# High and low words of h alternate in one tile, so that stationary columns lie 8 bytes apart

## The chip, the cores and the metric

One core of a Trainium2 chip runs the whole program. The metric is the device time of one execution in microseconds; for the kernel before, three runs gave a median of 735.1 us (735.01 to 736.07). An execution taken by the hardware profiler is what all rows below come from.

## The reference

Eight batches of 576 query rows and eight heads of width 64 go through two softmax attentions and then a gated feed-forward layer of width 1536 with three weight matrices:

```
p_packed = sm_attn(p, k, v)             # 32 rows per head
out      = sm_attn(q, p_packed, p_packed)
x        = out, as 4608 tokens x 512
g        = x @ w_gate
silu     = g * (1.0 / (1.0 + np.exp(-g)))
return   (silu * (x @ w_val)) @ w_out   # float32, 4608 x 512
```

`sm_attn` subtracts the row maximum, takes exp with scale 1/8, and divides by the sum plus 1e-9. The three weight matrices arrive as float64 and are made float32 on the chip.

## The kernel before

**What is multiplied.** The second attention is not applied to values first. Its probabilities (tile `a2`, 256 packed rows by 576 tokens of one batch) are multiplied with packed values that have gone through the weights (tile `m`). So a chunk of 128 columns of g, and one of the value branch, is m as stationary operand times a2 as moving operand, and comes out with the 128 feed-forward columns on the partitions and 256 or 320 tokens along the free axis. h = silu(g) * value has that layout too: 128 feed-forward columns by 256 tokens, and is the stationary operand of the output product, 128 tokens (columns of h) at a time, with 512 columns of w_out moving.

**High and low words.** To hold precision in TensorE's one-pass type float32r, a factor is split in a high word (the value rounded to float32r) and a low word (the rest). Each product is then three matmuls: low times high, high times low, high times high. For m and a2 the tiles are `mh`, `ml`, `a2h`, `a2l`; for w_out `wo_h`, `wo_l`; for h `hh`, `hl`.

**The loops.** `batch` (L904) runs over batches 1 to 7, and in it over 12 chunks of 128 feed-forward columns, each for a first part of the tokens (a) and a second (b), 256 and 320 columns wide. `gv_chunk` (L619) issues 6 matmuls in each of two PSUM banks (tag gv, two buffers, so a chunk's banks are also the next chunk's). Behind them ScalarE takes silu of the first bank (L640), VectorE multiplies it with the second (L644, for b a 64-column rest too, L647), and `h_split` (L610) makes the two words: ScalarE writes `hh` (the copy at L178), VectorE writes `hl` = h - hh (L614). `out_mm` (L650) multiplies them with w_out, three matmuls for each of two 128-token halves: (hl, wo_h), (hh, wo_l), (hh, wo_h). The output product of a chunk is issued one chunk of the same part later, so between the making of an h and its use stand an output product, the other part's chunk, another output product, and a chunk. The 64-token rests of two batches are collected in `t4`, split by VectorE alone (`split4`, tiles with tag 4, L180 and L614) and multiplied at the end of the odd batch into a bank named aux.

**What sets the order.** TensorE's order is as written (manual). For batch 0 a list of words (`PROGRAM`) sets the order on VectorE, ScalarE and SyncE too; there `h_high` and `h_low` make the words of the last two chunks, and earlier chunks use unsplit float32 (L828). From batch 1 on the attention of the next batches is put between the matmuls by tables (`FIRST`, `LATER`), called through `fill`. Some of these places put short matmuls, 32 columns of stationary operand wide, between a chunk and the output product behind it.

**The tiles that the change touches.** `hh` and `hl` are separate tiles of 128 x 256 float32r, three buffers each (`h_tile`, L607); with tag 4, two buffers each. They stand at consecutive addresses, and a stationary operand is 128 adjacent columns, 512 bytes in a row in each partition.

**Rows with a step of 8 bytes that are there already.** The weights come as pairs of 32-bit words. `f64_convert` (L191) reads high and low words of such pairs with a step of 8 bytes: L197 on ScalarE reads them and writes without gaps, L198 reads and writes with that step, L200 and L201 on VectorE have one operand with it and one without.

Of the kernel before, what the change touches and what calls it, by code (L numbers as in the profile page):

```python
# [11 lines left out]
F32R = mybir.dt.float32r  # L12
# [11 lines left out]
P = 128  # L24
# [108 lines left out]
def tile_pack_attention_swiglu(ctx: ExitStack, tc: tile.TileContext, qT, kT, v, vq, pT, wgv, wout, out):  # L133
# [5 lines left out]
    pool = ctx.enter_context(tc.tile_pool(name="pool", bufs=1))  # L139
# [24 lines left out]
    def pin(ins):  # L164

        return tc.keep_in_program_order(ins) if steady[0] else ins
# [9 lines left out]
    def copy(e, dst, src):  # L176
        if e is nc.scalar:
            e.copy(dst, src)  # L178
        else:
            e.tensor_copy(dst, src)  # L180
# [423 lines left out]

    t4 = {}

    def h_tile(t):  # L607
        return pool.tile([P, 256], F32R, tag=t, bufs=3, name=t)

    def h_split(src, hi, lo, between=lambda: False, tag=""):  # L610
        hh, hl = (pool.tile([P, 256], F32R, tag=t + tag, bufs=2, name=t) if tag else h_tile(t) for t in ("hh", "hl"))
        copy(hi, hh, src)
        last = between()
        low = lo.tensor_tensor(hl, src, hh.bitcast(F32), op=ALU.subtract)  # L614
        if last:
            pin(low)
        return hh, hl

    def gv_chunk(b, fc, is_b, fill, behind, between):  # L619
        odd = b % 2  # L620
        n = NB if is_b else NA
        off = (0 if odd else 256) if is_b else (320 if odd else 0)
        mh, ml = ms[b, fc // 2]
        ah, al = a2[b]
        f = fc % 2
        pgs = []
        for s in range(2):
            pg = ps_gv.tile([P, 512], F32, tag="gv", name="gv")
            pgs.append(pg)
            i = 0  # L630
            for m_, a_ in ((ml, ah), (mh, al), (mh, ah)):
                for g in range(NPAR):
                    nc.tensor.matmul(  # L633
                        pg[:, :n], m_[:, g, f, s * P : (s + 1) * P], a_[:, g, off : off + n],
                        start=(i == 0), stop=(i == 5),
                    )
                    i += 1
            fill()
        sg = pool.tile([P, NB], F32, tag="sg", bufs=1, name="sg")
        nc.scalar.activation(sg[:, :n], pgs[0][:, :n], AF.Silu)  # L640
        behind()
        hf = pool.tile([P, 256], F32, tag="hf", bufs=2, name="hf")
        o, o4 = (64, 0) if is_b and odd else (0, 256)
        nc.vector.tensor_tensor(hf, pgs[1][:, o : o + 256], sg[:, o : o + 256], op=ALU.mult)  # L644
        if is_b:
            r, r4 = slice(64 * odd, 64 * odd + 64), slice(o4, o4 + 64)
            nc.vector.tensor_tensor(t4[b // 2][:, fc, r], pgs[1][:, r4], sg[:, r4], op=ALU.mult)  # L647
        return h_split(hf, nc.scalar, nc.vector, between)
# [70 lines left out]
    with tc.manual_schedule(engines={mybir.EngineType.PE}):  # L719
# [19 lines left out]
        with tc.manual_schedule(  # L739
# [29 lines left out]
            hs = {}  # L769
# [42 lines left out]
                    nc.vector.tensor_tensor(t4[0][:, fc, :64], x[:, r], sg[:, r], op=ALU.mult)  # L812

            def h_high(i):
                hs[i].append(h_tile("hh"))
                nc.scalar.copy(hs[i][1], hs[i][0])

            def h_low(i):
                hs[i].append(h_tile("hl"))
                nc.vector.tensor_tensor(hs[i][2], hs[i][0], hs[i][1].bitcast(F32), op=ALU.subtract)  # L820

            def outs(i):
# [33 lines left out]
            def half_of(f, b):  # L856
# [5 lines left out]

            words = {
                "g": gv, "silu": silu, "h": hmul, "hh": h_high, "hl": h_low, "out": outs,
                "z_scores": lambda x: (None if x else s1_tile(0), s1_scores(0, x)), "z_max": lambda x: s1_max(0, x),
                "z_top": lambda x: s1_top(0), "z_exp": lambda x: s1_exp(0, True), "z_turn": lambda x: s1_turn(0, x),
# [21 lines left out]
            for word in PROGRAM.split():  # L888
                name = word[: word.index(":") + 1] if ":" in word else word.rstrip("0123456789")
# [14 lines left out]
        def batch(b, behind):  # L904
# [47 lines left out]
            def split4(*ks):  # L952
                for k in ks:
                    halves[k] = h_split(
                        t4_t[:, 2 * k : 2 * k + 2].rearrange("p f t -> p (f t)"), nc.vector, nc.vector, tag="4"
                    )
# [64 lines left out]
```

## Time and profile before

| | us |
|---|---|
| Median of three runs | 735.1 |
| The profiled execution, whole | 734.87 |
| Its span, first to last instruction | 733.1 |
| TensorE busy (6242 matmuls) | 723.9 |
| Loads of stationary operands busy (PEld, 6242) | 590.4 |
| VectorE busy | 454.2 |
| ScalarE busy | 373.7 |

So 1.8 us of the execution lie outside the span. TensorE's granted clock was 1.0 in all of it. In the profile's rows PE is a matmul, and PEld the load of its stationary operand, which overlaps the matmul before. Both last longer than the distance to the next one, since they are pipelined: what a matmul costs in a full stream is read from start to start, not from its duration. In the timeline, columns are start and duration in us, engine, line, operation, tile written from tiles read, and shape; a count of x2 merges two instructions. In groups, behind the bar stand busy time in us and mean ns of one, then idle time of the engine before them.

### The profile page before, as it was taken

Reading aid. Unit: us, or ns where it says so; the run is one execution under the profiler, and the core shown is the slowest. Engines: PE = TensorE matmul, PEld = TensorE weight load, DVE = VectorE, ACT = ScalarE, POOL = GpSimd, SP = SyncE. Lnnn points to the kernel's source line nnn. Section 1 sums busy time; section 2 is a strip of 40 time slices with the busy share of each in tenths; the row PEclk is TensorE's granted clock in tenths of the full one; section 3 lists DMA queues with packets and bytes.
Section 4 is the critical chain, followed back from the end, with each engine's and each line's share of the span. In section 5 each row is a group of like instructions: output and inputs, shape, how many; then the busy total and the mean of one; then the engine's idle time right before and its main releaser. Section 6 shows DMA issues by size and latency. Waiting matters only on the chain.

```text
span 733.1 us, 15099 instructions
## 1 busy us (share of the span) xinstructions
PE 723.9 (99%) x6242; PEld 590.4 (81%) x6242; DVE 454.2 (62%) x1009; ACT 373.7 (51%) x668; POOL 2.0 (0%) x13
## 2 busy tenths in 40 slices
PE   8899999999999999999999999999999999999997
PEld 4655667888888888888888888888888888888886
DVE  4999779665755557664764646665574655744333
ACT  3779737754635445553563535654453535533331
POOL 0000000000000000000000000000000000000000
PEclk9999999999999999999999999999999999999999
DMA  9697482310112201302112011102001000010001
GB/s 344 269 346 276 140 315 95 111 73 2 65 58 85 74 1 66 126 4 73 66 48 93 21 57 65 43 19 73 1 2 72 4 2 1 1 59 1 1 1 72
DMA packets 20004, 59.15 MB, mean 81 GB/s; under 512 B 5984, under 2 KB 7008, under 8 KB 17376
## 3 DMA queue, kind: packets, MB, share of 16 engines
q1 hardware_dynamic: 19792, 58.12, 21.9%
q8 instruction: 49, 0.80, 0.5%
q14 instruction: 19, 0.16, 0.1%
q10 hardware_dynamic: 144, 0.07, 0.0%
HBM read 48.69 MB, written 9.49 MB: 79 GB/s over the span
## 4 chain that ended last, share of the span: by engine, by line
PE 96%; DVE 1%; issue 0%; DVEq 0%
PE gv L633 36%; PE acc L652 34%; PE aux L267 7%; PE gv L787 6%; PE acc L828 5%; PE aux L652 4%; PE gv_aux L482 1%; PE gv_aux L398 1%; PE gv_aux L267 1%; DVE w L200 0%; PE acc L726 0%; PE aux L343 0%; DVE w L201 0%; PE aux L324 0%; DVE ot L180 0%; PE aux L398 0%
## 5 line engine op out<-in xcount | busy, mean ns | idle before, releaser
L640 ACT ACTIVATE sg<-gv 128x256 f32<-128x256 f32 (+1 forms) x168 | 69.0, 411 | 175.3 <-PE gv L633 161.6
L644 DVE TENSOR_TENSOR hf<-gv,sg 128x256 f32<-128x256 f32 x168 | 71.0, 422 | 129.8 <-PE gv L633 118.5
L633 PE MATMUL gv<-a2h,ml 128*128 128x256 f32 (+1 forms) x672 | 143.5, 295 | 0.0
L633 PE MATMUL gv<-a2l,mh 128*128 128x256 f32 (+1 forms) x672 | 143.4, 295 | 0.0
L633 PE MATMUL gv<-a2h,mh 128*128 128x256 f32 (+1 forms) x672 | 143.4, 295 | 0.0
L652 PE MATMUL acc<-wo_h,hl 128*128 128x512 f32 x344 | 139.8, 406 | 0.0
L652 PE MATMUL acc<-wo_l,hh 128*128 128x512 f32 x344 | 135.5, 394 | 0.0
L652 PE MATMUL acc<-wo_h,hh 128*128 128x512 f32 x344 | 135.5, 394 | 0.0
L633 PEld LDWEIGHTS gv<-a2h,ml 128*128 128x128 f32 x672 | 116.4, 189 | 15.3 <-ACT sg L803 0.4
L178 ACT CAST hh<-hf 128x256 fp32r<-128x256 f32 x168 | 67.7, 403 | 101.9 <-DVE hf L644 101.8
L633 PEld LDWEIGHTS gv<-a2l,mh 128*128 128x128 f32 x672 | 107.8, 189 | 0.0
L633 PEld LDWEIGHTS gv<-a2h,mh 128*128 128x128 f32 x672 | 107.6, 188 | 0.0
L614 DVE TENSOR_TENSOR hl<-hf,hh 128x256 fp32r<-128x256 f32 x168 | 69.8, 416 | 46.4 <-ACT hh L178 46.3
L652 PEld LDWEIGHTS acc<-wo_h,hl 128*128 128x128 f32 x344 | 64.5, 188 | 28.0 <-issue 19.2
L652 PEld LDWEIGHTS acc<-wo_h,hh 128*128 128x128 f32 x344 | 64.6, 188 | 14.6
L652 PEld LDWEIGHTS acc<-wo_l,hh 128*128 128x128 f32 x344 | 64.6, 188 | 8.3 <-issue 0.2
L571 DVE TENSOR_TENSOR ml<-aux,mh 128x512 fp32r<-128x512 f32 x92 | 58.9, 682 | 5.4 <-ACT mh L597 5.4
L267 PE MATMUL aux<-w,ppt 64*32 64x512 f32 (+1 forms) x784 | 52.1, 588 | 0.9 <-DVE w L201 0.9
L597 ACT CAST mh<-aux 128x512 fp32r<-128x512 f32 x92 | 49.4, 590 | 5.6 <-PE aux L267 1.2
L640 ACT ACT_TABLE_LOAD x30 | 38.5, 1283 | 13.6 <-PE gv L633 9.8
L828 PE MATMUL acc<-wo_f,h 128*128 128x512 f32 x80 | 37.8, 602 | 0.0
L828 PEld LDWEIGHTS acc<-wo_f,h 128*128 128x128 f32 x80 | 14.2, 189 | 16.7 <-issue 16.2
(153 smaller groups left out, 754.3 us busy)
## 6 DMA issues: line engine op xcount, KB each, us to landing
st<-in_wgv SPq DMA_DIRECT2D x12, 1024.0 KB, 7.6
k_t<-in_kT SPq DMA_DIRECT2D x16, 576.0 KB, 4.9
q_t<-in_qT SPq DMA_DIRECT2D x16, 576.0 KB, 4.9
out<-ot SPq DMA_DIRECT2D x36, 256.0 KB, 2.1
v_t<-in_vq SPq DMA_DIRECT2D x6, 1280.0 KB, 5.7
st<-in_wout SPq DMA_DIRECT2D x6, 1024.0 KB, 6.8
v_t<-in_v SPq DMA_DIRECT2D x2, 1024.0 KB, 8.7
p_t<-in_pT SPq DMA_DIRECT2D x7, 64.0 KB, 2.4
```

What stands on the lines that cost most here:

```text
L178: e.copy(dst, src)
L267: nc.tensor.matmul(outs[par][32 * hp : 32 * hp + 32], lhs(r, hp), rhs(r, hp), start=True, stop=True)
L398: nc.tensor.matmul(pss[par][NP * j : NP * j + NP, i * SQ : (i + 1) * SQ], p_t[r, 2 * g + i, :], k_t[r, j // 2, 2 * g + i, j % 2 * SQ : j % ...
L571: pin(nc.vector.tensor_tensor(*lows.pop(0), op=ALU.subtract))
L597: nc.scalar.copy(m[0][at], src)
L614: low = lo.tensor_tensor(hl, src, hh.bitcast(F32), op=ALU.subtract)
L633: nc.tensor.matmul(pg[:, :n], m_[:, g, f, s * P : (s + 1) * P], a_[:, g, off : off + n], start=(i == 0), stop=(i == 5),)
L640: nc.scalar.activation(sg[:, :n], pgs[0][:, :n], AF.Silu)
L644: nc.vector.tensor_tensor(hf, pgs[1][:, o : o + 256], sg[:, o : o + 256], op=ALU.mult)
L652: nc.tensor.matmul(acc[:, :], h_[:, c : c + P], w_[fc // 2][:, fc % 2], start=(fc == 0 and i == 0), stop=(fc == NFC - 1 and i == 2),)
L787: nc.tensor.matmul(held[i][s][:, :n], m_[:, g, f, s * P : (s + 1) * P], a_[:, g, off : off + n], start=(j == 0), stop=(j == len(todo) - 1),)
L828: nc.tensor.matmul(accs[2 * is_b + c], half(i)[:, c * P : c * P + P], wos[fc // 2][:, fc % 2], start=(fc == 0), stop=(fc == NFC - 1),)
```

## The change

The two words of h become two views of one tile of 128 x 256 x 2 elements: `x[:, :, 0]` is the high word, `x[:, :, 1]` the low word. Both have a step of 8 bytes from column to column. A stationary operand of 128 columns now spans 1024 bytes in each partition, of which it takes every other word. The tile with no tag has three buffers, that with tag 4 has two, so space and number of buffers stay as they were, and h starts at the same address; no other tile is moved.

```
-    def h_tile(t):
-        return pool.tile([P, 256], F32R, tag=t, bufs=3, name=t)
+    def h_tiles(tag=""):
+        x = pool.tile([P, 256, 2], F32R, tag="hx" + tag, bufs=2 if tag else 3, name="hx")
+        return x[:, :, 0], x[:, :, 1]
...
-        hh, hl = (pool.tile([P, 256], F32R, tag=t + tag, bufs=2, name=t) if tag else h_tile(t) for t in ("hh", "hl"))
+        hh, hl = h_tiles(tag)
...
             def h_high(i):
-                hs[i].append(h_tile("hh"))
+                hs[i].extend(h_tiles())
...
             def h_low(i):
-                hs[i].append(h_tile("hl"))
```

Each engine has the same instructions as before in the same order, with the same waits (source lines below the edit shift by one). What differs is the access pattern of 1568 of them: 1176 output matmuls read their stationary operand with the step; 172 copies on ScalarE and 24 on VectorE write the high word with it; 196 subtractions on VectorE read the high word and write the low word with it.

## The prediction

> **What bounds the kernel now.** I read the page first, for the span and the chain that ended last.
>
> ```profile
> span 733.1 us, 15099 instructions
> ...
> PE 96%; DVE 1%; issue 0%; DVEq 0%
> PE gv L633 36%; PE acc L652 34%; PE aux L267 7%; PE gv L787 6%; PE acc L828 5%; PE aux L652 4%; PE gv_aux L482 1%; PE gv_aux L398 1%; PE gv_aux L267 1%; DVE w L200 0%; PE acc L726 0%; PE aux L343 0%; DVE w L201 0%; PE aux L324 0%; DVE ot L180 0%; PE aux L398 0%
> ```
>
> TensorE is the chain. The output products (L652) are 38% of it, so the question is what a matmul costs there from start to start, and whether the load of its stationary operand can come to set that. The timeline of one output product and the chunk behind it shows the pace.
>
> ```profile
> 500.18 0.40 PE L652 MATMUL acc<-wo_h,hl 128*128 128x512 f32 x1
> ...
> 500.88 0.39 PE L652 MATMUL acc<-wo_h,hl 128*128 128x512 f32 x1
> 500.88 0.19 PEld L652 LDWEIGHTS acc<-wo_l,hh 128*128 128x128 f32 x1
> 501.10 0.39 PE L652 MATMUL acc<-wo_l,hh 128*128 128x512 f32 x1
> ...
> 501.56 0.40 PE L633 MATMUL gv<-a2h,ml 128*128 128x256 f32 x2
> 501.79 0.40 PE L633 MATMUL gv<-a2l,mh 128*128 128x256 f32 x2
> ```
>
> Six output matmuls take 501.56 - 500.18 = 1.38 us, 230 ns each. A chunk's 256-column matmul takes (501.79 - 501.56) / 2 = 115 ns. A load starts when the matmul before its own starts (both 500.88): it has that one matmul to hide under, no more.
>
> The groups give the length of a load by its columns (mean ns in the second place behind the bar), and the number of output matmuls.
>
> ```profile
> L652 PEld LDWEIGHTS acc<-wo_h,hl 128*128 128x128 f32 x344 | 64.5, 188 | 28.0 <-issue 19.2 <-DVE hf L809 0.2
> L652 PEld LDWEIGHTS aux<-wo_h,hl 128*128 128x128 f32 x48 | 9.0, 188 | 1.7
> L267 PEld LDWEIGHTS aux<-w,ppt 64*32 64x32 f32 x784 | 8.9, 104 | 9.1 <-DVE w L201 1.3 <-DVE wo_f L199 0.8 <-issue 0.7
> ```
>
> There are three such matmuls for each row: 3 x (344 + 48) = 1176. A load of 128 columns takes 188 ns and one of 32 takes 104, so a column costs (188 - 104) / 96 = 0.875 ns, 128 columns 112 ns, and 76 ns are fixed. The fixed part can overlap: at 256 columns loads follow each other every 115 ns. So of a load, 112 ns count against the matmul it hides under: 230 ns in an output product, but only about 115 when the first load of an output product hides under the last 256-column matmul of a chunk.
>
> **The change, part by part.** No instruction is added, removed or moved, and no wait differs; what can change is how long four kinds of instruction take.
>
> *Loads of h (1176).* No row of before has a stationary operand with gaps. The nearest rows are reads with the same step of 8 bytes on other engines, beside the same kind of work without gaps.
>
> ```profile
> L200 DVE SCALAR_TENSOR_TENSOR w<-w,st 128x1024 int32<-128x1024 int32 x12 | 14.6, 1222 | 0.5
> ...
> L233 DVE TENSOR_TENSOR wo_l<-wo_f,wo_h 128x512 fp32r<-128x512 f32 x12 | 8.2, 683 | 0.4
> ...
> L614 DVE TENSOR_TENSOR hl<-hf,hh 128x256 fp32r<-128x256 f32 x168 | 69.8, 416 | 46.4 <-ACT hh L178 46.3
> ...
> L197 ACT ACTIVATE w<-st 128x1024 f32<-128x1024 f32 x12 | 14.0, 1164 | 3.3 <-DMA st<-in_wgv 3.3
> ...
> L198 ACT ACTIVATE st<-st,minus_two 128x1024 f32<-128x1024 uint32 x18 | 22.5, 1260 | 0.0
> ...
> L229 ACT CAST wo_h<-wo_f 128x512 fp32r<-128x512 f32 x12 | 7.4, 613 | 1.5 <-DVE wo_f L201 1.5
> ...
> L178 ACT CAST hh<-hf 128x256 fp32r<-128x256 f32 x168 | 67.7, 403 | 101.9 <-DVE hf L644 101.8
> ```
>
> VectorE, two operands without gaps: (683 - 416) / 256 = 1.04 ns a column, which carried on to 1024 columns gives 683 + 512 x 1.04 = 1217 ns. L200, with one of its operands at the step, takes 1222. The read with the step is free there. The rate matters: VectorE takes a column every 1.04 ns, a load every 0.875 ns, which is near. ScalarE: (613 - 403) / 256 = 0.82 ns, at 1024 columns 1033; L197 with the read stepped takes 1164, or 13% more, L198 with read and write stepped 1260, 22% more (their functions differ, so part of this may be theirs). By these rows a load's 112 ns become 112 to 137. Under a 230 ns matmul either is hidden. I take VectorE's row, since it is a plain read of two streams as TensorE's is: 112 ns, no cost.
>
> [...]
>
> What a slower load would cost is seen where the cover is short. Here are the first loads of an output product behind short matmuls of the attention (546.40), and behind chunks of 256 and 320 columns.
>
> ```profile
> 546.40 0.19 PEld L652 LDWEIGHTS acc<-wo_h,hl 128*128 128x128 f32 x1 [0.23 <-issue]
> 546.40 0.50 PE L652 MATMUL acc<-wo_h,hl 128*128 128x512 f32 x1
> 546.51 0.19 PEld L652 LDWEIGHTS acc<-wo_l,hh 128*128 128x128 f32 x1
> ...
> 546.74 0.40 PE L652 MATMUL acc<-wo_l,hh 128*128 128x512 f32 x1
> ...
> 496.90 0.19 PEld L652 LDWEIGHTS acc<-wo_h,hl 128*128 128x128 f32 x1
> ...
> 497.02 0.39 PE L652 MATMUL acc<-wo_h,hl 128*128 128x512 f32 x1
> ...
> 549.51 0.19 PEld L652 LDWEIGHTS acc<-wo_h,hl 128*128 128x128 f32 x1
> ...
> 549.66 0.39 PE L652 MATMUL acc<-wo_h,hl 128*128 128x512 f32 x1
> ...
> PEld acc L652 <- issue: 19.4, 38, 0.8
> ```
>
> At 546.40 the load has no cover: the next matmul comes 0.34 us later, 0.11 more than the 0.23 elsewhere, which is the 112 ns of one load. The waits count 38 such places. Behind a chunk the cover is 0.12 us (496.90 to 497.02) or 0.15 (549.51 to 549.66). With 168 chunks (the count of L178) some 130 output products start that way, half with each.
>
> So a load with 137 ns costs 38 x 25 + 65 x 17 ns = 2.1 us. Twice the column time (224 ns) still hides inside an output product (230), and costs 38 x 112 + 65 x 104 + 65 x 74 ns = 15.8 us. Below nothing the bound is the 38 open loads: if they vanished, -4.3 us; but no column fewer is read, so I count no gain here.
>
> *Writing hh (172 on ScalarE).* Between nothing and 22% of 256 x 0.82 ns: up to 46 ns each. *Writing hl, reading hh (196 on VectorE).* The read is free by L200. A write with the step on VectorE has no row; I take nothing, as for the read, and as the upper end half rate, 256 x 1.04 = 267 ns more. Neither engine is on the chain; the place where an hl is used soonest, at the end of an even batch, and the end of the last batch show what cover they have.
>
> ```profile
> 551.38 0.39 ACT L178 CAST hh<-hf 128x256 fp32r<-128x256 f32 x1
> ...
> 551.81 0.43 DVE L614 TENSOR_TENSOR hl<-hf,hh 128x256 fp32r<-128x256 f32 x1 [1.32 <-ACT hh L178]
> ...
> 552.28 0.19 PEld L652 LDWEIGHTS acc<-wo_h,hl 128*128 128x128 f32 x1
> 552.43 0.40 PE L652 MATMUL acc<-wo_h,hl 128*128 128x512 f32 x1
> ...
> 726.63 0.29 DVE L180 CAST hh<-t 128x256 fp32r<-128x256 f32 x1 [0.61 <-PE aux L652]
> 726.96 0.43 DVE L614 TENSOR_TENSOR hl<-t,hh 128x256 fp32r<-128x256 f32 x1
> ...
> 727.79 0.39 PE L652 MATMUL aux<-wo_h,hl 128*128 128x512 f32 x1
> ```
>
> At 552.24 hl is done, 0.04 us before its load. With 46 + 267 ns more the matmul at 552.43 comes 0.28 us later: three even batches (2, 4, 6), 0.8 us. Batch 0 has its own list. At the end, hl is done at 727.39 and its matmul starts at 727.79, the load about 0.11 before: 0.29 us of cover. Here the copy (24 on VectorE, 0.29 us) could lose its pace too, at most to L614's 0.42, so 0.13 + 0.27 = 0.40 us, 0.11 over the cover, four times in each of four odd batches: 1.8 us. Elsewhere an h has a whole chunk and an output product more. So VectorE's writes are worth 0 to 2.6 us; I take 0.
>
> [...]
>
> The sum: 733.1 us span + 1.8 us around it (the profiled execution took 734.87) + 0 = 734.9, which is 0.2 below the median of the runs. I forecast the median: **735.1 us**. About 0.2%, 1.5 us, is what a measurement here can tell from no change.
>
> **The rivals.** *A, slower: the load of a column takes twice as long.* [...] The point from which it decides is the cover, 118 ns behind a 256-column chunk; from there each ns more costs 65 + 38 ns in all, up to 230 ns, where all 1176 matmuls would pay. At 224: 735.1 + 15.8 = 751. For it: no row shows a load with gaps, and ScalarE's rows are 13 to 22% up. Against it: VectorE's row.
>
> *B, slower by little.* VectorE's or ScalarE's writes with the step, or a load of 137 ns: 736.6 to 740.
>
> *C, faster: loads keep step with the moving operand.* Loads and moving columns are read at once. The end of the program shows output matmuls at another pace than the body:
>
> ```profile
> 720.99 0.39 PE L652 MATMUL aux<-wo_h,hl 128*128 128x512 f32 x1
> ...
> 728.92 0.39 PE L652 MATMUL aux<-wo_h,hh 128*128 128x512 f32 x1
> ```
>
> These are the first and the last of 36: 7.93 / 35 = 226.6 ns, against 230 in the body. If the 3.4 ns are the two reads meeting in memory, the change could take them away: a load now walks 8 bytes in 0.875 ns, the moving operand 4 bytes in 226.6 / 512 = 0.443 ns, both about 9 bytes a ns, where before one overtook the other. 1032 x 3.4 ns = 3.5 us, so 731.6. Against it: the matmuls at the end have the same loads of 128 columns without gaps and run at 226.6, so the 3.4 ns look like the other engines, which are mostly idle there. [...]
>
> *D, the change does not do what it says:* excluded, the 1176 access patterns differ.
>
> **How the numbers follow.** No change (734 to 736.6): 0.45. A (around 751): 0.18. B (736.6 to 740): 0.14. C (730.8 to 733.6, with the 4.3 us of the open loads as its far end): 0.23. So faster 0.23, same 0.45, slower 0.32. The range goes from C's far end, rounded to 730.5, to A's 751, with about half of A and little of C outside it: 730.5 to 751.
>
> **What would show it.** Right: the groups have L652's loads at 188 ns, L614 near 416 and L178 near 403 to 450, the output matmuls at 230 ns from start to start, and 0.34 us behind the load at a place like 546.40. A would show as loads of about 300 ns and the first matmul of an output product 70 to 100 ns late. B as L614 near 600 to 700 ns with the same loads. C as output matmuls at 227 ns in the body. Wrong altogether: chunk matmuls (L633) at another pace, since the change doesn't touch their operands.

## The result and the profile after

The changed kernel takes 738.5 us (median of 4, 738.35 to 739.64), the kernel before 735.06 (median of 4, 734.66 to 736.07) on the same chip: a ratio of 1.0048, with an interval of 1.0031 to 1.0066. It is slower by about half a per cent. I had forecast no change. The time lies in the range that I gave, and among the prices of rival B, but by a mechanism that B did not have.

The profiled execution took 738.35 us. The page of the kernel after gives its span and the chain.

```profile
span 736.6 us, 15099 instructions
...
PE 95%; DVE 1%; issue 0%; DVEq 0%
PE gv L634 36%; PE acc L653 34%; PE aux L267 7%; PE gv L788 5%; PE acc L828 5%; PE aux L653 5%; PE gv_aux L482 1%; PE gv_aux L398 1%; PE gv_aux L267 1%; DVE w L200 0%; PE acc L727 0%; PE aux L343 0%; DVE w L201 0%; PE aux L324 0%; DVE ot L180 0%; PE aux L398 0%
```

TensorE is the chain as before, and no new wait is in it. The span is 3.5 us longer (736.6 against 733.1). The groups of after answer to those of before for the four kinds of instruction that the change touches.

```profile
L653 PEld LDWEIGHTS acc<-wo_h,hx 128*128 128x128 f32 x688 | 133.0, 193 | 39.8 <-issue 19.2
L653 PEld LDWEIGHTS acc<-wo_l,hx 128*128 128x128 f32 x344 | 67.0, 195 | 7.0 <-issue 0.2
L178 ACT CAST hx<-hf 128x256 fp32r<-128x256 f32 x168 | 72.2, 430 | 102.1 <-DVE hf L645 102.0
L615 DVE TENSOR_TENSOR hx<-hf,hx 128x256 fp32r<-128x256 f32 x168 | 70.0, 416 | 48.2 <-ACT hx L178 48.0
```

A load takes 193 to 195 ns where it took 188, ScalarE's copy 430 where it took 403, VectorE's subtraction 416 as before. None of this is near the cover that the prediction counted. So look at the matmuls. These rows of the timeline of after are the first and the last of the same 36 matmuls at the end that rival C showed.

```profile
724.24 0.39 PE L653 MATMUL aux<-wo_h,hx 128*128 128x512 f32 x1
...
732.41 0.40 PE L653 MATMUL aux<-wo_h,hx 128*128 128x512 f32 x1
```

(732.41 - 724.24) / 35 = 233.4 ns from start to start, where it was 226.6. Each matmul there is 6.8 ns later than the one before it, though its load (about 195 ns) is well inside.

The first chunk matmul (L787, after L788) shows how much of the 3.5 us was lost before the main work: here in before, then in after.

```profile
24.43 1.96 PE L787 MATMUL gv<-a2f,mh 128*128 128x256 f32 x8 [1.05 <-DVE a2f L756]
```

```profile
25.15 1.89 PE L788 MATMUL gv<-a2f,mh 128*128 128x256 f32 x8
```

It starts 0.72 us later, at the end of the loading stage, which the change doesn't touch. In the profiled execution of after the granted clock was 0.50 from 12 to 18 us, where it was 1.0 in before. The mean granted clock of the whole profiled execution is 0.995 in after and 1.0 in before; of the experiments e1_writes (0.995) and g2_shift64 (0.994) are as low, and are 0.7 us late too; the others have 0.998 to 1.0 and lie from 0.6 us early to 0.5 us late. From there to the last matmul it is 732.41 - 25.15 = 707.26 us, against 728.92 - 24.43 = 704.49: 2.77 us more, and these are the change's. For them I summed the distances from each matmul's start to the next one's over all records, by the tile and the columns that stream. The table has before in us, and the difference to it for after and for nine of the experiments below; its aux column holds the products with w_out alone.

| | acc, 512 col. (1112) | aux, 512 col. (143) | chunk, 256 col. (1136) | chunk, 320 col. (1136) |
|---|---|---|---|---|
| before | 274.70 | 32.58 | 144.75 | 172.34 |
| after | +1.42 | +0.75 | -0.35 | +0.87 |
| e1_writes | +0.11 | 0.00 | -0.12 | +0.10 |
| e2_loads | +1.40 | +0.75 | -0.27 | +0.81 |
| e4_step0 | +0.41 | +0.57 | -0.02 | +0.33 |
| f1_shift | +0.04 | +0.83 | -0.07 | +0.01 |
| f2_shift8 | +1.51 | +0.61 | -0.28 | +0.83 |
| g1_all32 | +2.59 | +0.83 | -1.19 | +0.14 |
| g2_shift64 | +2.08 | +0.67 | -0.05 | +0.18 |
| h1_shift8b | -0.69 | +0.51 | +0.12 | +0.26 |
| h2_mh192 | -0.02 | 0.00 | +1.42 | +0.23 |

In after the four columns make 2.69 of the 2.77 us. Output products have 2.17 of it (the acc column holds the 80 unsplit float32 matmuls of batch 0 too; four of these in a row in before take 38.18 - 36.46 = 1.72 us, 430 ns each, where one of float32r takes 230). Of the +1.42 into acc, 0.43 stands at 43 output matmuls whose load has no cover, 0.63 at 693 inside an output product in the body, and 0.32 at 163 that have a chunk behind them. The chunk columns have the other 0.52, though the change doesn't touch their operands. The last matmul of a chunk has a load of h beside it, but these have only 0.17 of the 0.52; the rest lies at other places of a chunk, and its cause is open.

### The profile page after: what moved, and what is told of

Read it like the earlier page. It is cut to its first block, busy times and chain, and to the rows that moved or that the text cites. A ratio compares the mean times of both kernels' runs of the same rounds, so it can differ in the third digit from the quotient of the medians.

```text
span 736.6 us, 15099 instructions
## 1 busy us (share of the span) xinstructions
PE 728.7 (99%) x6242; PEld 598.9 (81%) x6242; DVE 454.2 (62%) x1009; ACT 377.8 (51%) x668; POOL 2.0 (0%) x13
## 4 chain that ended last, share of the span: by engine, by line
PE 95%; DVE 1%; issue 0%; DVEq 0%
PE gv L634 36%; PE acc L653 34%; PE aux L267 7%; PE gv L788 5%; PE acc L828 5%; PE aux L653 5%; PE gv_aux L482 1%; PE gv_aux L398 1%; PE gv_aux L267 1%; DVE w L200 0%; PE acc L727 0%; PE aux L343 0%; DVE w L201 0%; PE aux L324 0%; DVE ot L180 0%; PE aux L398 0%
## 5 line engine op out<-in xcount | busy, mean ns | idle before, releaser
L653 PE MATMUL acc<-wo_h,hx 128*128 128x512 f32 x688 | 247.2, 401 | 0.0
L653 PEld LDWEIGHTS acc<-wo_h,hx 128*128 128x128 f32 x688 | 133.0, 193 | 39.8 <-issue 19.2
L653 PE MATMUL acc<-wo_l,hx 128*128 128x512 f32 x344 | 135.4, 394 | 0.0
L178 ACT CAST hx<-hf 128x256 fp32r<-128x256 f32 x168 | 72.2, 430 | 102.1 <-DVE hf L645 102.0
L615 DVE TENSOR_TENSOR hx<-hf,hx 128x256 fp32r<-128x256 f32 x168 | 70.0, 416 | 48.2 <-ACT hx L178 48.0
L653 PEld LDWEIGHTS acc<-wo_l,hx 128*128 128x128 f32 x344 | 67.0, 195 | 7.0 <-issue 0.2
L653 PE MATMUL aux<-wo_h,hx 128*128 128x512 f32 x96 | 31.2, 394 | 0.0
L198 ACT ACTIVATE st<-st,minus_two 128x1024 f32<-128x1024 uint32 x18 | 22.7, 1267 | 0.0
```

Source lines behind the costliest of these rows:

```text
L198: yield nc.scalar.activation(lo.bitcast(F32), lo.bitcast(U32), AF.Identity, bias=minus_two, scale=LOW_WORD)
L653: nc.tensor.matmul(acc[:, :], h_[:, c : c + P], w_[fc // 2][:, fc % 2], start=(fc == 0 and i == 0), stop=(fc == NFC - 1 and i == 2),)
```

## The experiments

**The theories.** Writes: the copies and subtractions with the step delay something. Longer load (L): the 6 ns of a load reach the matmul. Spread (S): a load costs the running matmul more where its words lie further apart. Meeting (P): what a load takes from the matmul beside it depends on how the two reads, of stationary and of moving words, meet in the addresses. For P the addresses in the built program matter: a w_out operand starts in each partition at 192 bytes modulo 512, and an operand of h, before, at 448, so that both are equal modulo 256. In after the first word of h is still there.

### Writes alone, loads alone

e1_writes has the tile and the writes of the change, and loads of 128 adjacent words. It thus multiplies by a mixture of high and low words.

```
-                h_[:, c : c + P],
+                next(f for v, f in flats if v is h_)[:, 2 * c + P * (i > 0) : 2 * c + P * (i > 0) + P],
```

> The words of h are written with the step of 8 bytes, but the output products load 128 adjacent words of that tile (so they multiply a mixture of words; the output is not the reference's). Theory S (spread: a load takes time from the matmul it lies beside, and the more, the further its columns are spread): loads at 188 ns, output matmuls 226.7 ns apart in the quiet last stretch and 230 in the body, copy of hh still 430 ns, time as before, 735 us. Rival W (the stepped writes, of which the copy of hh grew from 403 to 430 ns, disturb TensorE or come late): 738 us. Rival L (a load is itself 6 ns longer and pushes the matmul behind it, the pace of 226.7 being the moving operand's own): as S here, 735.

It took 735.49 us, a ratio of 1.0005 (0.9997 to 1.0014). Groups and timeline of e1_writes:

```profile
L657 PEld LDWEIGHTS acc<-wo_h,hx 128*128 128x128 f32 x688 | 129.1, 188 | 42.7 <-issue 19.2 <-DVE hf L814 0.2
L178 ACT CAST hx<-hf 128x256 fp32r<-128x256 f32 x168 | 72.2, 430 | 102.1 <-DVE hf L649 102.0
```

```profile
721.83 0.39 PE L657 MATMUL aux<-wo_h,hx 128*128 128x512 f32 x1
...
729.76 0.39 PE L657 MATMUL aux<-wo_h,hx 128*128 128x512 f32 x1
```

The copy has its 430 ns, and the pace is 7.93 / 35 = 226.6 ns as before. The writes cost nothing.

e2_loads writes hh and hl as before, and loads every second word of them, so that its stationary operands are other columns of h than the product needs.

```
-                h_[:, c : c + P],
+                h_[:, c // P :: 2],
```

> The kernel before, with hh and hl in separate tiles and written without gaps, but the output products load every second word of the 256 (wrong columns; the output is not the reference's). Theory S: loads 194 ns, output matmuls 233.3 ns apart in the last stretch, 233 in the body, 738 us, the whole of the change's cost. Rival W: 735 us, loads 188 ns. Rival L: as S, 738.

It took 737.86 us, 1.0040 (1.0026 to 1.0053). Groups and timeline of e2_loads:

```profile
L652 PEld LDWEIGHTS acc<-wo_l,hh 128*128 128x128 f32 x344 | 67.0, 195 | 7.0 <-issue 0.2
L178 ACT CAST hh<-hf 128x256 fp32r<-128x256 f32 x168 | 67.7, 403 | 102.1 <-DVE hf L644 102.0
```

```profile
723.74 0.39 PE L652 MATMUL aux<-wo_h,hl 128*128 128x512 f32 x1
...
731.91 0.40 PE L652 MATMUL aux<-wo_h,hh 128*128 128x512 f32 x1
```

8.17 / 35 = 233.4 ns: with the loads alone the whole loss is there, and its row in the table is that of after.

### Wider and narrower steps

e3_step16 interleaves the two 128-token halves as well, so that a load has a step of 16 bytes.

```
-        x = pool.tile([P, 256, 2], F32R, tag="hx" + tag, bufs=2 if tag else 3, name="hx")
-        return x[:, :, 0], x[:, :, 1]
+        x = pool.tile([P, P, 4], F32R, tag="hx" + tag, bufs=2 if tag else 3, name="hx")
+        return tuple(x[:, :, i::2].rearrange("p n c -> p c n") for i in range(2))
```

> The changed kernel with the two 128-column halves alternating too, so that a load's columns are 16 bytes apart in the same space (same output as the reference). Theory S: the step from 4 to 8 bytes cost 6.7 ns a matmul in the quiet stretch, so 16 bytes costs at least twice that again, 13 ns more than the change, 246 ns apart or more, 1176 x 13 ns = 16 us, 754 us or above. Rival L: another 6 ns of load, 239 ns apart, 745 us. Rival W: 738 to 740.

It took 759.82 us, 1.0334 (1.0320 to 1.0348). Its groups, and the start of an output product behind a chunk:

```profile
L654 PEld LDWEIGHTS acc<-wo_h,hx 128*128 128x128 f32 x688 | 200.0, 310 | 20.6 <-issue 19.2 <-DVE hx L616 1.0 <-DVE hx L821 0.2
L178 ACT CAST hx<-hf 128x256 fp32r<-128x256 f32 x168 | 112.0, 667 | 105.6 <-DVE hf L646 105.6
L616 DVE TENSOR_TENSOR hx<-hf,hx 128x256 fp32r<-128x256 f32 x168 | 104.8, 624 | 69.6 <-ACT hx L178 69.4
```

```profile
566.40 0.45 PE L635 MATMUL gv<-a2h,mh 128*128 128x320 f32 x2
566.69 0.49 PE L654 MATMUL acc<-wo_h,hx 128*128 128x512 f32 x1
567.01 0.40 PE L654 MATMUL acc<-wo_l,hx 128*128 128x512 f32 x1
567.25 0.64 PE L654 MATMUL acc<-wo_h,hx 128*128 128x512 f32 x2
```

At 16 bytes the load itself is long: 310 - 76 = 234 ns for 128 columns, 1.83 ns each. This is the load that rival A had (224 ns), and a delay like A's is seen: the second matmul of a product comes 0.32 us behind the first (566.69 to 567.01), the next 0.24. At 8 bytes there is nothing of it, so the change's loss is another thing than this. Theory S had forecast such a time (754 us or above), but by a pace of 246 ns or more at the end of the program; it is 235.5 ns into acc there and 244 into aux.

f4_step12 is the changed kernel with loads that take every third word (a step of 12 bytes, so other words than the product needs).

```
-                h_[:, c : c + P],
+                next(f for v, f in flats if v is h_)[:, c // 2 : c // 2 + 3 * P : 3],
```

> Words written with the step of 8 bytes as in e1_writes, loads with a step of 12 bytes (a mixture of words; the output is not the reference's). Theory S: between the steps of 8 and 16 bytes: loads 200 to 300 ns, output matmuls 234 ns or more in the quiet stretch, 741 to 758 us. If a load's time only turns at 16 bytes: loads 200 ns, 738 to 742 us.

It took 746.56 us, 1.0160 (1.0144 to 1.0175). The group of f4_step12:

```profile
L657 PEld LDWEIGHTS acc<-wo_h,hx 128*128 128x128 f32 x688 | 170.3, 252 | 19.7 <-issue 19.2 <-DVE hf L814 0.2
```

The load lies between: (252 - 76) / 128 = 1.38 ns a column. So in these runs a column costs 0.875, 0.92, 1.38 and 1.83 ns at steps of 4, 8, 12 and 16 bytes: at 8 bytes the step is nearly free for the load (0.05 ns a column), and at 12 and 16 bytes each 4 bytes more cost about 0.45 ns.

e4_step0 loads one column 128 times; the output is made of that column of h alone.

```
-                h_[:, c : c + P],
+                h_[:, c : c + 1].broadcast_to([P, P]),
```

> The kernel before, but each load of an output product reads one column 128 times (step 0; the output is not the reference's). [...] Rival L (226.7 ns is the moving operand's own pace): still 226.7 ns, 735 us. Rival W: 735 us.

It took 736.65 us, 1.0018 (1.0009 to 1.0027). Timeline of e4_step0:

```profile
722.66 0.40 PE L652 MATMUL aux<-wo_h,hl 128*128 128x512 f32 x1
...
730.77 0.39 PE L652 MATMUL aux<-wo_h,hh 128*128 128x512 f32 x1
```

8.11 / 35 = 231.7 ns, slower than before's 226.6, with loads of 188 ns. Theory S falls here: a load that reads no more than one word in each partition had to be the cheapest by it. Rival L, by which the pace stays at 226.7, missed too. From the same start address the matmuls come every 226.6 ns with a step of 4 bytes, and every 231.7 and 233.4 ns with steps of 0 and of 8 bytes.

### The start address

f1_shift is the kernel before, with 256 bytes of unused tile ahead of h. One other tile is made smaller, so that the tiles with tag 4 (for aux) are moved by 32 bytes only. No step is changed. Here, and wherever below a tile named pad is added, four other tiles that lie behind h move too (t2, z1, ot, x1); none of them is an operand of an output product.

```
+        if not pads:
+            pads.append(pool.tile([P, 64], F32, tag="pad", bufs=1, name="pad"))
+            nc.gpsimd.memset(pads[0], 0.0)
```

> The kernel before with hh and hl 256 bytes further (so that they lie as w_out does, modulo 512 bytes), and the tag-4 tiles 32 bytes further. Theory P (what a load takes from the matmul beside it depends on how the addresses of the two reads meet): the output matmuls' pace in the quiet last stretch moves from 226.7 ns by some ns, in its first part (acc) or its second (aux), and the time by up to 1176 x 7 ns = 8 us. Theory S (spread alone): 226.7 ns in both parts, 735 us.

It took 735.75 us, 1.0014 (1.0005 to 1.0022). Timeline of f1_shift, the last twelve matmuls into acc, and the 36 into aux behind them:

```profile
718.87 0.39 PE L660 MATMUL acc<-wo_h,hl 128*128 128x512 f32 x1
...
721.37 0.40 PE L660 MATMUL acc<-wo_h,hh 128*128 128x512 f32 x1
721.60 0.39 PE L660 MATMUL aux<-wo_h,hl 128*128 128x512 f32 x1
...
729.76 0.40 PE L660 MATMUL aux<-wo_h,hh 128*128 128x512 f32 x1
```

Into acc (h moved by 256 bytes) they come every 2.50 / 11 = 227 ns, as in before; into aux (moved by 32 bytes) every 8.16 / 35 = 233.1 ns. It is the same kernel, a moment apart, with the same loads. In the table its loss is in the aux column alone: +0.83 us.

g1_all32 moves all tiles of h by 32 bytes in the kernel before, by an unused tile of 32 bytes.

```
+        if not pads:
+            pads.append(pool.tile([P, 8], F32, tag="pad", bufs=1, name="pad"))
+            nc.gpsimd.memset(pads[0], 0.0)
```

> The kernel before (words without gaps, loads without gaps) with all tiles of hh and hl 32 bytes further. Theory P (what a load takes from the matmul beside it depends on how its addresses meet those of the moving operand, and the step of 8 bytes was only one way to a bad meeting): 233.2 ns in both parts of the quiet stretch, 232 to 233 in the body, loads still 188 ns, 738 us, as slow as the change without any step. Rival S2 (the 32 bytes matter only for the tiles with tag 4, the step is what slows the rest): first part 226.7, second 233.2, 735.8 us.

It took 737.70 us, 1.0037 (1.0024 to 1.0049). Group and timeline of g1_all32:

```profile
L657 PEld LDWEIGHTS acc<-wo_l,hh 128*128 128x128 f32 x344 | 64.8, 188 | 8.3 <-issue 0.2
```

```profile
723.57 0.40 PE L657 MATMUL aux<-wo_h,hl 128*128 128x512 f32 x1
...
731.74 0.40 PE L657 MATMUL aux<-wo_h,hh 128*128 128x512 f32 x1
```

233.4 ns, with adjacent words and loads of 188 ns: the kernel before, moved by 32 bytes, is as slow as the changed one within their intervals. So this pace needs no longer load (L). The loss is made up in another way than that of after: +3.42 us in the output products and -1.05 at the chunks, where after has +2.17 and +0.52.

f2_shift8 is the changed kernel with the edit of f1, so moved by 256 bytes for h and by 32 with tag 4.

```
-        x = pool.tile([P, NJ + 6, 2, H], F32, tag="x1", bufs=1, name="x1")[:, :NJ]
+        x = pool.tile([P, 104], F32, tag="x1", bufs=1, name="x1")[:, :64].rearrange("p (j s h) -> p j s h", j=NJ, s=2)
...
+            pads.append(pool.tile([P, 64], F32, tag="pad", bufs=1, name="pad"))
```

> The changed kernel with the same shift of addresses. Theory P: another pace than 233.3 ns in the quiet stretch; with the 8-byte step both reads advance at about the same rate, so a shift should matter most here, and 226.7 or less would be possible at some address. Theory S: 233.3 ns, 738 us.

It took 737.14 us, 1.0032 (1.0020 to 1.0045). Into acc the pace is 233.3 ns as in after, into aux 231.9: with the step of 8 bytes, 256 bytes more still change nothing, where theory P had expected another pace.

g2_shift64 moves h by 64 bytes and tag 4 by -128 in the kernel before.

```
-        x = pool.tile([P, NJ + 6, 2, H], F32, tag="x1", bufs=1, name="x1")[:, :NJ]
+        x = pool.tile([P, 112], F32, tag="x1", bufs=1, name="x1")[:, :64].rearrange("p (j s h) -> p j s h", j=NJ, s=2)
...
+            pads.append(pool.tile([P, 16], F32, tag="pad", bufs=1, name="pad"))
```

> The kernel before with hh and hl 64 bytes further and the tag-4 tiles 128 bytes lower. Theory P with a period of 64 bytes: 226.7 ns in both parts, 735 us. P with a period of 256 bytes: one or both parts at another pace, up to 233 ns, up to 738 us.

It took 737.49 us, 1.0034 (1.0021 to 1.0048; its first chunk matmul was 0.7 us late in the profile). Timeline of g2_shift64:

```profile
724.36 0.39 PE L657 MATMUL aux<-wo_h,hl 128*128 128x512 f32 x1
...
732.49 0.40 PE L657 MATMUL aux<-wo_h,hh 128*128 128x512 f32 x1
```

The pace is 233.1 ns into acc and 232.4 into aux. Of the moves tried without a step, 0 and 256 bytes are good (226.6 and 227 ns), and 32, 64 and -128 are not (232.4 to 233.4 ns).

h1_shift8b is the changed kernel with these same two lines, and so the same moves.

```
+            pads.append(pool.tile([P, 16], F32, tag="pad", bufs=1, name="pad"))
...
         x = pool.tile([P, 256, 2], F32R, tag="hx" + tag, bufs=2 if tag else 3, name="hx")
```

> The changed kernel with hx 64 bytes further and the tag-4 tiles 128 bytes lower. Theory P in its plain form (only the meeting counts, the step can meet well too): somewhere 226.7 ns, here or at the starts tried before. If the step itself costs: 231 to 234 ns in both parts of the quiet stretch at every start, 737 to 739 us.

It took 735.10 us, 1.0005 (0.9995 to 1.0014). Group and timeline of h1_shift8b:

```profile
L658 PEld LDWEIGHTS acc<-wo_h,hx 128*128 128x128 f32 x688 | 133.8, 195 | 39.1 <-issue 19.2 <-DVE hf L815 0.2
```

```profile
721.30 0.40 PE L658 MATMUL aux<-wo_h,hx 128*128 128x512 f32 x1
...
729.40 0.40 PE L658 MATMUL aux<-wo_h,hx 128*128 128x512 f32 x1
```

The loads are as long as in after or longer (195 ns), the pace at the end is 231.4 ns into aux and 230.1 into acc, and the acc column is 0.69 us below before's. The step is there and its net cost is gone: +0.51 us into aux and +0.59 at the 43 loads without cover are made up by -0.89 inside the output products of the body (230.4 ns on average instead of 231.7) and -0.38 at their last matmuls. This is not faster than before, but as fast. It is faster than the same moves without the step: g2 took 737.49 us, 2.4 us more. Neither expectation came in full, since no part has 226.7 ns and the time is not 737 us or above.

h2_mh192 tries the rule on the chunk products: in the kernel before, m's high words are moved by 192 bytes, so that they start as the moving a2 does modulo 256 (modulo 512 in half of the products); two unused tails of tiles make the room.

```
-            pool.tile([P, 6 * NPAR * NBK + 52], F32, tag="r2", bufs=1, name="r2")[:, : 6 * NPAR * NBK].rearrange(
+            pool.tile([P, 6 * NPAR * NBK + 100], F32, tag="r2", bufs=1, name="r2")[:, : 6 * NPAR * NBK].rearrange(
...
-            t4[b // 2] = pool.tile([P, NFC * P + 48], F32, tag="t4", bufs=1, name="t4")[:, : NFC * P].rearrange(
+            t4[b // 2] = pool.tile([P, NFC * P], F32, tag="t4", bufs=1, name="t4")[:, : NFC * P].rearrange(
```

> The kernel before with the tiles mh moved up by 192 bytes, so that they start as a2h and a2l do, modulo 512 bytes (two pads change by 48 words, no step anywhere). Theory P with a period of 256 bytes, as in f1_shift and g2_shift64: chunk matmuls beside loads of mh come to 144 ns for 320 columns and 115 for 256, from 146 and 118, so 1344 x 2 to 3 ns = 2.7 to 4 us less, 731 to 732 us. If the rule is the output products' own: 735 us, same pace as before.

It took 736.67 us, 1.0026 (1.0016 to 1.0035). The 256-column matmuls of a chunk come every 120 ns instead of 118 (medians over 1040 of each kernel), and their column has +1.42 us; the output products' columns are unchanged. So addresses matter for chunks too, but "equal starts are best", by which P had 731 to 732 us, does not hold there, and the rule behind it is not known.

### How much a load takes

f3_half loads 64 columns for two of three matmuls, in the kernel before; half of their output rows are left out.

```
+            n = P if i == 2 or (fc == 0 and i == 0) else P // 2
...
-                acc[:, :],
-                h_[:, c : c + P],
+                acc[:n, :],
+                h_[:, c : c + n],
```

> The kernel before, but two of the three loads of an output product take 64 columns in place of 128 (the other 64 rows get no low-word terms; the output is not the reference's). [...] Rival L (226.7 is the moving operand's own pace): 226.7 ns, 735 us.

It took 732.53 us, 0.9969 (0.9957 to 0.9981). The group of f3_half:

```profile
L653 PEld LDWEIGHTS acc<-wo_l,hh 128*64 128x64 f32 x344 | 46.4, 135 | 17.4 <-issue 0.3
```

A load of 64 columns takes 135 ns, as 76 + 64 x 0.875 = 132 has it. But at the end of the program the pace is 229.6 ns, not below 226.7: fewer loaded words did not make the matmul beside them faster there. Of the 2.7 us that the acc products gain, 1.8 are at the 43 loads without cover, where the next matmul comes after 294 ns instead of 336 on average; inside the output products of the body the pace is 230.6 ns instead of 231.7. The 226.7 ns of L are not seen.

g3_n384 streams 384 of the 512 columns for two of three matmuls (the other columns lack these terms).

```
+            n = DM if i == 2 or (fc == 0 and i == 0) else 384
...
-                acc[:, :],
+                acc[:, :n],
...
-                w_[fc // 2][:, fc % 2],
+                w_[fc // 2][:, fc % 2, :n],
```

> The kernel before, but two of the three matmuls of an output product stream 384 of the 512 columns (the last 128 columns of the output get no low-word terms; it is not the reference's). If 226.7 ns is the moving operand's own pace and nothing of it the load's: 384 x 226.7 / 512 = 170.0 ns from start to start in the quiet stretch. [...]

It took 707.22 us, a single run. Timeline of g3_n384 in the quiet end:

```profile
695.05 0.34 PE L653 MATMUL aux<-wo_h,hl 128*128 128x384 f32 x1
695.23 0.34 PE L653 MATMUL aux<-wo_l,hh 128*128 128x384 f32 x1
695.40 0.40 PE L653 MATMUL aux<-wo_h,hh 128*128 128x512 f32 x1
695.64 0.33 PE L653 MATMUL aux<-wo_h,hl 128*128 128x384 f32 x1
```

Two 384-column matmuls and one of 512 take 0.59 us; over the 36 into aux it is 176 and 178 ns for the two, and 232 ns for the third. The 170.0 ns did not come, so it is not shown that 226.7 ns is the moving operand's own pace. And the matmul of 512 columns took 232 ns instead of 226.6, though its operands and the load beside it are as in before. So the distance depends on the neighbours as well. How much of it is the load's stays open, since no run has these matmuls without a load.

## Why the prediction failed

**The step that failed** is "Under a 230 ns matmul either is hidden. ... 112 ns, no cost." A load's own time is hidden, as I said: 193 to 195 ns of 233. But I took hidden for free, and put what the load takes from the matmul that hides it at nothing. The two overlap (in before a load and the matmul that hides it both start at 500.88 us), and the runs show that the matmul's pace changes with nothing but the step (e2) or the start address (f1, g1) of the load. In before it had the lowest pace that any run with full loads showed at the end of the program, 226.6 ns from start to start; with the step, at the same start address, it has 233.4. That is 6.8 ns for each output matmul there. In the body it is far less, since before had no good pace there: 231.7 ns on average inside the output products, and 232.6 after. In all it is +1.42 us over 1112 matmuls into acc (0.43 of it at the loads without cover, where the longer load counts), +0.75 into aux and +0.52 at the chunks, 2.69 of the 2.77 us. The runs show it from both sides: g1 has a cost of this size without the step, h1 the step without the cost. How the load slows the matmul is not shown, and neither is that it takes the meeting of two addresses: w_out, the moving operand, lay at the same place in every run.

**Rival C** asked about the right quantity and had the wrong sign. I asked whether the two reads keep step, at about 9 bytes a ns each; with the step they about do (a load takes 8 bytes in 0.92 ns), and the pace at the end got worse. What I set against C was that "the matmuls at the end have the same loads ... and run at 226.6, so the 3.4 ns look like the other engines". That may be so: what makes the body of before slower than its end I have not tried. But I read from it that loads are not in question, and the 226.6 ns were lost in f1 by a move of 32 bytes alone.

**The load: right in the bounds.** 118 ns of it count (194 - 76), where I said 112 to 137 and took 112. At the loads without cover the next matmul came 346 instead of 336 ns later on average, 43 places, 0.43 us, which is inside the acc column. The prediction had 38 places and 25 ns each as the upper price. It also took the products behind a chunk as half behind each kind; 84 stand behind a chunk of 320 columns and 42 behind one of 256.

**The writes: right.** The subtraction stayed at 416 ns, so the write with a step of 8 bytes is free on VectorE. The copy on ScalarE went from 403 to 430 ns, where I allowed up to 46 ns more, and nothing waits for it: e1 shows both at no cost.

**Rival A**'s factor of two was my estimate. It does not hold at 8 bytes (118 ns for 128 columns, not 224), and does at 16 (234), with one of the signs that I gave it, loads of about 300 ns. I had the first matmul of a product late by 70 to 100 ns; it was the second, by 95 ns behind chunks of 320 columns and by 124 behind those of 256 (326 and 355 ns behind the first instead of 231). Its 15.8 us were too little: e3 took 24.6 us more than before, with a load 10 ns longer than A's and slower writes.

**Rival B** had the time, 736.6 to 740, and by luck: its writes cost nothing, and its longer load makes 0.4 us at most. **The sign of "wrong altogether"**, chunk matmuls at another pace, hardly showed: the median distances are 118 ns at 256 columns and 147 at 320 in both, while the two sums moved by -0.35 and +0.87 us.

**The chances.** The mistake was to weigh only durations. The two paces, 226.6 and 230, stood in the profile of before and said that the same matmul, with a load of the same length beside it, can take 3.4 ns more or less. I looked for a way to win these, and gave no chance to losing as many by the same means.

## What to carry to other kernels

In these runs a load that was covered in time (193 to 195 ns of 233) still slowed the matmul that covered it (233.4 ns from start to start instead of 226.6), so read the pace from start to start over a long quiet stretch, where 3% show that no group's mean shows. What it is worth is then read from the body: 6.8 ns at the end of this program were 0.9 ns inside the output products before it. When a layout of an operand is changed, try the kernel before with its operands moved by 32 and 64 bytes as a control, before the layout is blamed or praised: here the address alone was worth as much as the whole change. In these runs steps of up to 8 bytes cost the load of a stationary operand almost nothing (194 ns instead of 188), and steps of 12 and 16 bytes much (252 and 310 ns); at 16 bytes VectorE (624 ns instead of 416) and ScalarE (667 instead of 403) are slower as well.

## What the runs showed that I had not expected

- At the end of the program, the pace of 512-column float32r matmuls, each with a full load of 128 adjacent words beside it, depends on the load's start address: 226.6 to 227 ns for h at its place in before and 256 bytes on, 232.4 to 233.4 ns at 32, 64 and -128 bytes. The instructions that read h and w_out are the same in all of them. Whether the address counts by itself or against that of w_out was not tried.
- With a step of 8 bytes the addresses matter in another way there: 233.3 to 233.4 ns at 0 and 256 bytes, 231.9 at 32, 230.1 at 64, 231.4 at -128. No address tried with the step reached 226.7.
- A load that reads one column 128 times takes 188 ns, as one of 128 adjacent columns does, and its matmuls come every 231.7 ns.
- At a step of 16 bytes ScalarE's copy took 667 ns instead of 403, and VectorE's subtraction 624 instead of 416.
